# Decayed attention, a folded double product and routed experts on one core: the first combined product ahead of the last value products, and remainders on VectorE piece by piece

## The chip, the cores and the metric

The kernel runs on one core of a Trainium2 chip. The core has a matmul engine (TensorE, PE in the profile), three elementwise engines (VectorE, DVE; ScalarE, ACT; GpSimd, POOL) and SyncE (SP), whose queue issues the transfers that matter here. Each engine works through its own instructions in their order, and semaphores order the engines among each other. SBUF is the on-chip memory of 128 partitions, PSUM the banks that matmuls accumulate in. The metric is the device time of one launch in microseconds (us).

## What is computed

Attention over 4 batches of 8 heads, 576 tokens and 64 columns, with a decay from `f`; its output is the input x of a product of weights, and that the input of a layer with 8 experts. The reference, cut to what matters:

```python
cum = np.cumsum(np.log(np.clip(f, 0.0001, 1.0)), axis=-1)
scores = np.where(causal, -1e9, scale * q @ k.T + cum[:, None] - cum[None, :])
attn = np.exp(scores - scores.max(-1)); attn /= attn.sum(-1) + 1e-09
x = (attn @ v)                      # 2304 tokens x 512
a = x @ w1                          # w1, w2: 512 x 1024
b = x @ w2
h = a * b @ w3                      # 1024 x 1024
x = h @ w_out                       # 1024 x 512
# then: each token to the best of 8 experts, relu(x @ w1[e]) @ w2[e], scaled by its gates
```

## The kernel before

**Stages.** Attention works on 16 pairs of two heads (4 batches, 4 pairs each). A table, `START`, gives each step of a pair a due time in a period of 9.8, and steps of neighbouring pairs are written out in the order of those times; `AFTER` holds exceptions for the last pairs. Behind attention come the combined matrix C = w3 · w_out, the gated stage (a = x·w1, b = x·w2, their product, 8 column blocks f by 5 tiles of 512 tokens), the projection of that with C, the routing, and the experts.

**Products.** Every float32 matmul is done as three matmuls on rounded halves: hi·hi, hi·lo, lo·hi (lines 515 to 517, and 552 to 554 for the gated stage). C is 16 products (`hf`, j): two halves of its rows by 8 slices of the inner dimension, each of 12 matmuls of 128x512. The order is (0,0) to (0,3), (1,0) to (1,3), then (0,j), (1,j) for j = 4 to 7. At the end of each half its four PSUM banks (`wc`) are evicted, by ACT the `hi` (line 770) and by DVE the remainder (line 771). The first products of the gated stage are a00, b00, a01, b01 (tile 0, block f).

**Pieces.** The weights lie in DRAM as 64-bit words. `narrow` turns a piece of 128x512 into two halves of float32 in seven steps: 0 SP loads it (512 KB, line 449) into one of three buffers (tag `raw`); 1 ACT makes a scaled copy of the upper words (456); 2, 3, 4 DVE shifts and merges bits in place (458, 460, 462; 462 is the last to read the load buffer); 5 ACT rounds to `hi` (465); 6 POOL takes the remainder `lo` (467), or DVE where the argument `lows` says so. The pieces come in the order of the products: wo0, w00, wo1, ... (the first 12), then wo4, w04, w14, wo5, w05, w15, and so on to w17 (wo: slice j of w_out; w0j, w1j: of w3), then wa0, wb0, wa1, wb1, ... (blocks of w1 and w2). The tile that a piece has behind step 1 is called after it with a u: wo6u, w05u. Behind attention `convert` writes the steps of neighbouring pieces into the engines' queues, by a list of (step, how far ahead of the piece that is finished); `xsplit` does hi and remainder of the first tile of x (lines 572 and 573) between them.

**Ends of attention.** For a pair `pv` issues the value products (line 306), `add_blocks` adds probabilities on POOL (`ac`, line 297), `sums` brings their sums into the same PSUM tile (line 322), and `keep_sums` copies them out. At a batch's last pair `invert` loads the batch's sums (`z`, line 342), inverts them on DVE (344, 345) and stores them (`rz`, line 347).

Of the kernel before, what the change touches and what calls it, by code (L numbers as in the profile page):

```python
# [11 lines left out]
F32 = mybir.dt.float32  # L12
# [4 lines left out]
ALU = mybir.AluOpType  # L17
# [5 lines left out]
B, H, S, D = 4, 8, 576, 64  # L23
# [5 lines left out]
P = 128  # L29
# [9 lines left out]
AHEAD = 2  # L39

EARLY = 12
LOADS = 4

BLOCK = [(0, 192), (128, 832), (256, 1280), (384, 0), (512, 768)]
WIDTH = 1600
# [17 lines left out]

AFTER = {
    "K4_13": 4.4, "K4_14": 4.43, "K0_15": 15.6, "K0_16": 15.61, "K0_17": 15.62, "inputs": 11.36, "scores": 13.38,
    "K1_15": 18.5, "K1_16": 18.51, "K4_15": 18.52, "K0_18": 18.53, "K4_16": 18.54, "P0": 28.29, "P1": 28.3, "P2": 28.31,
    "P3": 28.32,
}

# [1 line left out]
def spread(nc, d, rz):  # L71

    for h in range(2):
        nc.sync.dma_start(out=d[64 * h:64 * h + 64], in_=rz[h:h + 1].broadcast_to([64, rz.shape[1]]))


def attention(nc, tc, ident, xT, rz, xs, wc, q, k, v, f):
# [6 lines left out]
    V, A, G, PE, SP = nc.vector, nc.scalar, nc.gpsimd, nc.tensor, nc.sync  # L84
    with (
# [70 lines left out]
        z = p1.tile([P, 512], BF16, name="warm")  # L156
# [16 lines left out]
        def tl(s, key, shape, dt=F32, bufs=2):  # L173
            if key in ("kh", "kl"):
                s[key] = KHs[key == "kl"][s["n"] % 2]
                return s[key][:, :S]
            if key not in s:
                pool = p2 if key in ("qr", "kr", "kh", "kl", "qh", "ql") else p3
                s[key] = pool.tile([P, *shape], dt, name=f"{key}_{s['n']}", tag=key, bufs=bufs)
            return s[key]  # L180
# [151 lines left out]
            b, pr = divmod(s["n"], NP)  # L332
            SP.dma_start(out=zd[pr, :, S * b:S * b + S].rearrange("h (i c) -> h i c", i=2), in_=s["zs"][0:P:32])

        def invert(s, step):

            if s["n"] % NP == NP - 1:
                b = s["n"] // NP
                z = tl(s, "z", (36,))
                view = lambda t: t.rearrange("x h n -> (x h) n")[:, S * b:S * b + S].rearrange("r (i c) -> r i c", c=36)  # L340
                if step == 0:
                    SP.dma_start(out=z, in_=view(zd))
                elif step == 1:
                    V.tensor_scalar(out=z, in0=z, scalar1=1e-9, scalar2=None, op0=ALU.add)
                    V.reciprocal(z, z)
                else:
                    SP.dma_start(out=view(rz), in_=z)
# [64 lines left out]
class Combined:  # L412


    def __init__(self, nc, tc, xpool, raw, wo, w3t):
        self.nc, self.tc, self.xpool, self.wo, self.w3t = nc, tc, xpool, wo, w3t
        self.pieces = [("o", 0), (0, 0), ("o", 1), (0, 1), ("o", 2), (0, 2), ("o", 3), (0, 3), (1, 0), (1, 1), (1, 2), (1, 3)]
        self.steps = [(hf, j) for hf in range(2) for j in range(4)]
        for j in range(4, 8):
            self.pieces += [("o", j), (0, j), (1, j)]  # L420
            self.steps += [(0, j), (1, j)]
        self.at = {x: i for i, x in enumerate(self.pieces)}
        self.queue = [self.narrow(f"w{x}{j}", wo[j] if x == "o" else w3t[x, j], self.slot(i)) for i, (x, j) in enumerate(self.pieces)]
        self.done, self.acc, self.spare = [0] * 7, {}, None
        self.raw = [raw.tile([P, 8, 512], F32, name=f"raw{i}", tag="u") for i in range(2)]
        self.units = [None] * 3
# [51 lines left out]
    def convert(self, n):  # L478

        for _ in range(n):  # L480
            x = self.done[6]
            for step, ahead in ((0, LOADS), (6, 1), (1, 4), (4, 2), (3, 3), (2, 4)):
                self.upto(step, x + ahead)

    def two(self, part):
# [34 lines left out]
def moe(nc, tc, ident, xT, rz, xs, xpool, raws, region, wc, w1, w2, gates, e1, e2, out):  # L520

    V, A, G, PE, SP = nc.vector, nc.scalar, nc.gpsimd, nc.tensor, nc.sync
    NCH = N // P
    with (
# [16 lines left out]
        def tmp(name):  # L541
            return st["work"].tile([P, 512], F32, name=name, tag="tmp", bufs=TMP if "moa" in st else 3)

        def split(src, hi, lo, lo_eng):
            G.tensor_scalar(out=hi, in0=src, scalar1=1.0, scalar2=1.0, op0=ALU.mult, op1=ALU.mult)  # L545
            lo_eng.tensor_tensor(out=lo, in0=src, in1=hi.bitcast(F32), op=ALU.subtract)  # L546
# [11 lines left out]
        def xparts(t):  # L558
            return [st["moa"].tile([P, 4, 512], F32R, name=f"{x}{t}", tag=x) for x in ("xh", "xl")]

        def xsplit(t, w, x, ks=range(4)):
            xh, xl = x
            for k in ks:
                xv = xT[:, k, 512 * t:512 * t + w]
                if t:
                    d = tmp(f"rz{t}{k}")[:, :w]
                    spread(nc, d, rz[k, :, 512 * t:512 * t + w])
                    G.tensor_tensor(out=xv, in0=xv, in1=d, op=ALU.mult)
                if t:
                    split(xv, xh[:, k, :w], xl[:, k, :w], V)  # L570
                else:
                    A.activation(out=xh[:, k, :w], in_=xv, func=ACTF.Copy)
                    G.tensor_tensor(out=xl[:, k, :w], in0=xv, in1=xh[:, k, :w].bitcast(F32), op=ALU.subtract)

        def gated(t, w, x, between):

# [170 lines left out]
        for f in range(8):  # L747
            for x, src, hi, lo in (("a", w1, w1h, w1l), ("b", w2, w2h, w2l)):
                spare = f % 2 if x == "b" and f > 1 else None
                wc.queue.append(wc.narrow(f"w{x}{f}", src[f], lambda hi=hi[:, f], lo=lo[:, f]: (hi, lo), spare, V if f else None))  # L750
        wc.banks(1, side="right")
        for hf, j in wc.steps:
            need = max(wc.at[hf, j], wc.at["o", j]) + 1
            wc.convert(max(0, need + AHEAD - wc.done[6]))
            if hf and j == 5:
                wc.first.close()
                st["moa"] = xpool.enter_context(tc.tile_pool(name="moa", bufs=1, side="right", reuse_waits="tile"))
                x = xparts(0)
            wc.product(hf, j)
            ks = XS.get((hf, j), ())  # L760
            if ks:
                xsplit(0, 512, x, ks)
            if 3 in ks:
                wc.spare = [xT[:, k:k + 2, 0:512] for k in (0, 2)]
            if j == 7:
                if hf == 0:
                    wch, wcl = (x.bitcast(F32R) for x in wc.raw)
                    st["unit"] += 2
                for f, ps in enumerate(wc.acc[hf]):
                    A.activation(out=wch[:, 4 * hf + f], in_=ps, func=ACTF.Copy)  # L770
                    V.tensor_tensor(out=wcl[:, 4 * hf + f], in0=ps, in1=wch[:, 4 * hf + f].bitcast(F32), op=ALU.subtract)  # L771
# [5 lines left out]
        gated(0, TT[0], x, iter(()))  # L777
        x = xparts(1)
        xsplit(1, TT[1], x)


# [31 lines left out]
        with tc.manual_schedule(engines={PE_E, POOL_E}):  # L813
            for t, w in list(enumerate(TT))[1:]:
# [3 lines left out]
                if t + 1 < len(TT):  # L818
                    x = xparts(t + 1)
# [290 lines left out]
        with tc.manual_schedule(engines={PE_E, DVE_E}):  # L1110
# [40 lines left out]
            x = next(fx)  # L1151
# [12 lines left out]
            for i in range(1, E):  # L1164
                nm, w = str(i), WIN[i]
# [17 lines left out]
                x = next(fx, None)  # L1183
# [9 lines left out]
                else:  # L1193
                    x = turned_piece("p", g2)
# [39 lines left out]
def program(shapes):  # L1234
    nc = bacc.Bacc("TRN2", target_bir_lowering=False, num_devices=1)
    a = {n: nc.dram_tensor(n, s, mybir.dt.from_np(t), kind="ExternalInput").ap() for n, (s, t) in shapes.items()}
    out = nc.dram_tensor("out", (N, DM), F32, kind="ExternalOutput").ap()
    with tile.TileContext(nc) as tc:
        with tc.tile_pool(name="keep", bufs=1) as keep, tc.tile_pool(name="raws", bufs=2, reuse_waits="tile") as raws, tc.tile_pool(name="div", bufs=1, space=DRAM) as div:
            rz = div.tile([NP, 2, N], F32, name="rz")  # L1240

            xs = div.tile([E * N, DM + 2], F32, name="xs")
            ident = keep.tile([P, P], F32, name="ident")
            keep.tile([P, 64], F32, name="shift")
            make_identity(nc, ident)
            xpool = ExitStack()
            xt = xpool.enter_context(tc.tile_pool(name="xt", bufs=1, side="right"))
            xT = xt.tile([P, NP, N], F32, name="xT")
            region = ExitStack()
            region.enter_context(tc.manual_schedule())  # L1250
            wc = Combined(nc, tc, xpool, raws, a["wo"], a["w3t"])
            attention(nc, tc, ident, xT, rz, xs, wc, a["q"], a["k"], a["v"], a["f"])
            moe(nc, tc, ident, xT, rz, xs, xpool, raws, region, wc, a["w1"], a["w2"], a["gates"], a["e1"], a["e2"], out)
            xpool.close()
    return nc
# [9 lines left out]
```

## Time and profile before

| what | value |
|---|---|
| median of 3 runs | 809.11 us (806.85 to 809.75) |
| the profiled execution | 808.69 us, of it the span 807.0 us |
| PE busy in the span | 778.8 us, 97% |
| DVE busy | 456.1 us, 57% |
| ACT, POOL busy | 280.0 us, 344.3 us |
| mean granted clock of PE | 0.997 of full speed |

The span runs from the profile's first instruction to its last; the execution's own time has what lies around it too. A row of a timeline gives start and duration, the engine, the line of the kernel, the operation, output and inputs, and in brackets how long the engine had been idle before it and what ended that.

### The profile page before, as it was taken

To read this page: it belongs to the slowest core of one execution; us is meant where nothing else is said; L and a number is where in the kernel's file an instruction comes from. 1 tells how busy PE (TensorE), PEld (TensorE's weight loads), DVE (VectorE), ACT (ScalarE), POOL (GpSimd) and SP (SyncE) were. 2 spreads that over 40 slices of the span, in tenths; PEclk is the share of its full clock that TensorE was granted. 3 is DMA by queue.
4 is the path that set the end of the run, shared out by engine and by line. 5 is a ranking of instruction groups with operands and counts; after the bars stand their busy time and mean duration, and the time that the engine had idled before them with its cause. 6 is when DMAs were issued, how large, how long until landed. Compare 5 with 4: busy or idle time off the path is not lost.

```text
span 807.0 us, 13835 instructions
## 1 busy us (share of the span) xinstructions
PE 778.8 (97%) x5171; PEld 644.0 (80%) x5173; DVE 456.1 (57%) x971; ACT 280.0 (35%) x536; POOL 344.3 (43%) x362
## 2 busy tenths in 40 slices
PE   8999999998999999999999999999899999999995
PEld 4666666676878887887888788898698999999983
DVE  7788888986899833340341322237367845446520
ACT  2566666553366412212222221223122222332221
POOL 6788888987460130230121011033445444443521
PEclk9999999999999999999999999999999999999998
DMA  3555767524545210110100010044676556456470
GB/s 108 164 161 182 229 213 242 155 61 144 171 170 185 78 41 14 53 39 1 53 16 17 21 40 0 2 132 144 205 230 212 173 194 198 166 189 222 143 264 29
DMA packets 40339, 102.12 MB, mean 127 GB/s; under 512 B 8610, under 2 KB 9314, under 8 KB 40016
## 3 DMA queue, kind: packets, MB, share of 16 engines
q1 hardware_dynamic: 37088, 91.46, 35.7%
q0 software_dynamic: 3184, 9.77, 3.2%
q8 instruction: 41, 0.67, 0.3%
q14 instruction: 26, 0.21, 0.1%
HBM read 84.47 MB, written 16.51 MB: 125 GB/s over the span
## 4 chain that ended last, share of the span: by engine, by line
PE 63%; DVE 14%; DMA 10%; issue 6%; POOL 4%; ACT 2%; SPq 0%; POOLq 0%; DVEq 0%; ACTq 0%
DVE junk L243 6%; PE b L552 4%; PE y L552 4%; PE y L554 4%; PE b L554 4%; PE a L552 4%; PE b L553 4%; PE y L553 4%; PE a L554 4%; PE a L553 4%; DMA out<-ot,id 3%; PE h L552 3%; PE h L554 3%; PE h L553 3%; POOL ac L297 2%
## 5 line engine op out<-in xcount | busy, mean ns | idle before, releaser
L582 DVE TENSOR_TENSOR ga<-b,ga 128x512 f32<-128x512 f32 (+1 forms) x40 | 25.4, 634 | 143.5 <-PE b L554 142.8
L711 POOL DMA_INDIRECT xs<-xr,pos x18 | 19.3, 1074 | 177.6 <-DVE pos L707 127.7
L243 DVE CUSTOM_DVE_ANT_0 junk<-x,tri 128x256 f32<-128x256 f32 (+3 forms) x128 | 62.6, 489 | 9.9 <-PE x L217 0.7
L552 PE MATMUL h<-gh,ah 128*128 128x320 f32 (+4 forms) x224 | 67.2, 300 | 0.0
L553 PE MATMUL h<-gl,ah 128*128 128x320 f32 (+4 forms) x224 | 66.9, 299 | 0.0
L554 PE MATMUL h<-gh,al 128*128 128x320 f32 (+4 forms) x224 | 66.9, 299 | 0.0
L552 PE MATMUL b<-xh,w2h 128*128 128x512 f32 (+1 forms) x160 | 60.1, 376 | 0.4 <-DVE raw L771 0.4
L552 PE MATMUL a<-xh,w1h 128*128 128x512 f32 (+1 forms) x160 | 59.8, 374 | 0.0
L554 PE MATMUL a<-xh,w1l 128*128 128x512 f32 (+1 forms) x160 | 59.1, 369 | 0.0
L554 PE MATMUL b<-xh,w2l 128*128 128x512 f32 (+1 forms) x160 | 59.0, 369 | 0.0
L553 PE MATMUL b<-xl,w2h 128*128 128x512 f32 (+1 forms) x160 | 58.9, 368 | 0.0
L553 PE MATMUL a<-xl,w1h 128*128 128x512 f32 (+1 forms) x160 | 58.8, 368 | 0.0
L285 POOL TENSOR_SCALAR_AFFINE_SELECT PT<-PT 128x256 f32<-128x256 f32 (+1 forms) x80 | 45.7, 586 | 28.7 <-ACT PT L279 26.5
L552 PE MATMUL y<-raw,gh 128*128 128x512 f32 x144 | 56.8, 395 | 0.0
L554 PE MATMUL y<-raw,gl 128*128 128x512 f32 x144 | 56.2, 390 | 0.0
L553 PE MATMUL y<-raw,gh 128*128 128x512 f32 x144 | 56.0, 389 | 0.0
L545 POOL TENSOR_SCALAR bh<-rb 128x1024 fp32r<-128x1024 f32 x28 | 35.7, 1277 | 47.4 <-DMA rb<-e 40.6
L584 ACT ACTIVATE gh<-ga 128x512 fp32r<-128x512 f32 (+1 forms) x40 | 23.6, 589 | 89.5 <-DVE ga L582 89.5
L991 DVE SCALAR_TENSOR_TENSOR hl<-h,hh 128x320 fp32r<-128x320 f32 (+4 forms) x56 | 25.5, 463 | 47.9 <-ACT hh L990 47.2
L306 PE MATMUL v<-PT,vr 128*64 128x448 f32 (+4 forms) x384 | 49.8, 396 | 1.1 <-ACT zs L329 1.1
L297 POOL TENSOR_TENSOR ac<-ac,PT 128x640 f32<-128x640 f32 (+1 forms) x32 | 45.6, 1424 | 1.6
L546 DVE TENSOR_TENSOR bl<-rb,bh 128x1024 fp32r<-128x1024 f32 x28 | 36.8, 1336 | 15.4 <-POOL bh L545 15.4
(611 smaller groups left out, 2165.8 us busy)
## 6 DMA issues: line engine op xcount, KB each, us to landing
ra<-e SPq DMA_DIRECT2D x28, 512.0 KB
rb<-e SPq DMA_DIRECT2D x28, 512.0 KB
w<-w3t SPq DMA_DIRECT2D x16, 512.0 KB
xs<-zero SPq DMA_DIRECT2D x8, 771.0 KB
vr<-v SPq DMA_DIRECT2D x16, 320.0 KB
kr<-k SPq DMA_DIRECT2D x16, 288.0 KB
qr<-q SPq DMA_DIRECT2D x16, 288.0 KB
wo<-wo SPq DMA_DIRECT2D x8, 512.0 KB
```

Source lines behind the costliest of these rows:

```text
L243: V.tensor_tensor_reduce(out=junk[:, :w], in0=s["x", i][:, 512 * h:512 * h + w] if i < 4 else s["x", i][:, 224:224 + S], in1=tri[:, 640 - ...
L285: G.affine_select(out=t, in_=t, pattern=[[0, 2], [1, w]], compare_op=ALU.is_ge, fill=0.0, base=0, channel_multiplier=-1,)
L297: G.tensor_tensor(out=acc[:, :, q0 - P:], in0=first if j == 1 else acc[:, :, q0 - P:], in1=src, op=ALU.add)
L306: PE.matmul(s["v"][HALF[h], 384 + q0:384 + q1], s["vr"][:, j, HALF[h]], place(s, j, h, q0, q1), start=(j == 0), stop=(j == 4 or q1 == P),)
L545: G.tensor_scalar(out=hi, in0=src, scalar1=1.0, scalar2=1.0, op0=ALU.mult, op1=ALU.mult)
L546: lo_eng.tensor_tensor(out=lo, in0=src, in1=hi.bitcast(F32), op=ALU.subtract)
L552: PE.matmul(ps, ah, bh, start=start and i == 0, stop=False)
L553: PE.matmul(ps, ah, bl, start=False, stop=False)
L554: PE.matmul(ps, al, bh, start=False, stop=stop and i == last)
L582: V.tensor_tensor(out=ga[:, :w], in0=pb[:, :w], in1=ga[:, :w], op=ALU.mult)
L584: A.activation(out=gh[:, f, :w], in_=ga[:, :w], func=ACTF.Copy)
L991: V.scalar_tensor_tensor(out=hl[:, f, :w], in0=ps[:, :w], scalar=0.0, in1=hh[:, f, :w].bitcast(F32), op0=ALU.max, op1=ALU.subtract)
```

## The change

Line numbers of the changed kernel are 3 to 5 higher: 458, 460, 462 become 461, 463, 465; 456 becomes 459; 465 and 467 become 468 and 470; 515 to 517 become 518 to 520; 770 and 771 become 775 and 776.

1. The first combined product (due time `P0`) is due at 22.9 and not at 28.29, just ahead of `p0` at 22.91, the first of the value products. It applies to the last pair alone.
2. The remainders of the pieces from wo4 on, of wa0 and wb0, and of x's first tile go to DVE; before, POOL took them.
3. `convert` has another list, and `LOADS` is 5: DVE's three steps and the remainder of a piece come one after another.
4. The last batch's sums are loaded into a tile that is kept, and DVE's inverse and the store of `rz` come at product (0,4).

```diff
-LOADS = 4
+LOADS = 5
...
-    "K1_15": 18.5, "K1_16": 18.51, "K4_15": 18.52, "K0_18": 18.53, "K4_16": 18.54, "P0": 28.29, "P1": 28.3, "P2": 28.31,
+    "K1_15": 18.5, "K1_16": 18.51, "K4_15": 18.52, "K0_18": 18.53, "K4_16": 18.54, "P0": 22.9, "P1": 28.3, "P2": 28.31,
...
-        def invert(s, step):
+        def invert(s, step, late=False):
...
-                z = tl(s, "z", (36,))
+                z = tl(s, "z", (36,)) if b < B - 1 else wc.last
...
+                elif b == B - 1 and not late:
+                    wc.late = lambda: (invert(s, 1, True), invert(s, 2, True))
...
-        self.queue = [self.narrow(f"w{x}{j}", wo[j] if x == "o" else w3t[x, j], self.slot(i)) for i, (x, j) in enumerate(self.pieces)]
+        self.queue = [self.narrow(f"w{x}{j}", wo[j] if x == "o" else w3t[x, j], self.slot(i), None, nc.vector if i >= 12 else None) for i, (x, j) in enumerate(self.pieces)]
...
-            for step, ahead in ((0, LOADS), (6, 1), (1, 4), (4, 2), (3, 3), (2, 4)):
+            for step, ahead in ((6, 1), (1, 4), (4, 2), (5, 2), (0, LOADS)):
...
-                    G.tensor_tensor(out=xl[:, k, :w], in0=xv, in1=xh[:, k, :w].bitcast(F32), op=ALU.subtract)
+                    V.tensor_tensor(out=xl[:, k, :w], in0=xv, in1=xh[:, k, :w].bitcast(F32), op=ALU.subtract)
...
-                wc.queue.append(wc.narrow(f"w{x}{f}", src[f], lambda hi=hi[:, f], lo=lo[:, f]: (hi, lo), spare, V if f else None))
+                wc.queue.append(wc.narrow(f"w{x}{f}", src[f], lambda hi=hi[:, f], lo=lo[:, f]: (hi, lo), spare, V))
...
+            if (hf, j) == (0, 4):
+                wc.late()
...
-            keep.tile([P, 64], F32, name="shift")
+            last = keep.tile([P, 64], F32, name="last")[:, :36]
```

The first place is PE's queue at the end of attention; `v` is the PSUM tile of a pair (2676 is pair 14's, 2739 or 2751 pair 15's), `cw` holds the first pieces. Before:

```order
L322 MATMUL v_2676<-PT_2543,ones 32x64 x2
L306 MATMUL v_2739<-PT_2659,vr_2695 64x128 x2
L306 MATMUL v_2739<-PT_2659,vr_2695 64x448 x4
L306 MATMUL v_2739<-PT_2659,vr_2695 64x320 x2
L306 MATMUL v_2739<-PT_2659,vr_2695 64x192 x2
L306 MATMUL v_2739<-PT_2659,vr_2695 64x64 x2
L322 MATMUL v_2739<-ac_2718,ones 32x288 x2
```

The twelve matmuls of product (0,0) stood behind the last of pair 15's sums. The same queue now:

```order
L322 MATMUL v_2676<-PT_2543,ones 32x64 x2
L518 MATMUL wc_2687<-cw 128x512
L519 MATMUL wc_2687<-cw 128x512
L520 MATMUL wc_2687<-cw 128x512
L518 MATMUL wc_2688<-cw 128x512
```

They stand between pair 14's sums and pair 15's value products.

The second place is DVE's queue in the middle of the conversion, around the pieces wo6 and w06. Before:

```order
L458 TENSOR_SCALAR wo6u<-wo6u 128x512
L462 SCALAR_TENSOR_TENSOR w15u<-w_2732,w15u 128x512
L460 SCALAR_TENSOR_TENSOR wo6u<-wo_2910,wo6u 128x512
L458 TENSOR_SCALAR w06u<-w06u 128x512
L462 SCALAR_TENSOR_TENSOR wo6u<-wo_2910,wo6u 128x512
L460 SCALAR_TENSOR_TENSOR w06u<-w_2931,w06u 128x512
L458 TENSOR_SCALAR w16u<-w16u 128x512
L462 SCALAR_TENSOR_TENSOR w06u<-w_2931,w06u 128x512
```

Now:

```order
L461 TENSOR_SCALAR wo6u<-wo6u 128x512
L463 SCALAR_TENSOR_TENSOR wo6u<-wo_2904,wo6u 128x512
L465 SCALAR_TENSOR_TENSOR wo6u<-wo_2904,wo6u 128x512
L470 TENSOR_TENSOR gl<-wo6u,gl 128x512
L461 TENSOR_SCALAR w06u<-w06u 128x512
L463 SCALAR_TENSOR_TENSOR w06u<-w_2913,w06u 128x512
L465 SCALAR_TENSOR_TENSOR w06u<-w_2913,w06u 128x512
L470 TENSOR_TENSOR gl<-w06u,gl 128x512
```

Three pieces were in work at a time; now a piece is done whole, its remainder among its steps.

The third place is DVE's queue from wb0 to the combined product's second eviction (`wc_2687` and the three behind it are the banks of the first half, `wc_2841` or `wc_2845` the first of the second; w2l is wb0's remainder). Before:

```order
L462 SCALAR_TENSOR_TENSOR wb0u<-wb_3043,wb0u 128x512
L460 SCALAR_TENSOR_TENSOR wa1u<-wa_3066,wa1u 128x512
L458 TENSOR_SCALAR wb1u<-wb1u 128x512
L771 TENSOR_TENSOR raw_78<-wc_2687,raw_77 128x512
L771 TENSOR_TENSOR raw_78<-wc_2688,raw_77 128x512
L771 TENSOR_TENSOR raw_78<-wc_2689,raw_77 128x512
L771 TENSOR_TENSOR raw_78<-wc_2690,raw_77 128x512
L462 SCALAR_TENSOR_TENSOR wa1u<-wa_3066,wa1u 128x512
L460 SCALAR_TENSOR_TENSOR wb1u<-wb_3075,wb1u 128x512
L458 TENSOR_SCALAR wa2u<-wa2u 128x512
L771 TENSOR_TENSOR raw_78<-wc_2845,raw_77 128x512
```

Now:

```order
L465 SCALAR_TENSOR_TENSOR wb0u<-wb_3024,wb0u 128x512
L576 TENSOR_TENSOR xl_2995<-xT,xh_2994 128x512
L776 TENSOR_TENSOR raw_78<-wc_2687,raw_77 128x512
L776 TENSOR_TENSOR raw_78<-wc_2688,raw_77 128x512
L776 TENSOR_TENSOR raw_78<-wc_2689,raw_77 128x512
L776 TENSOR_TENSOR raw_78<-wc_2690,raw_77 128x512
L470 TENSOR_TENSOR w2l<-wb0u,w2h 128x512
L461 TENSOR_SCALAR wa1u<-wa1u 128x512
L463 SCALAR_TENSOR_TENSOR wa1u<-wa_3049,wa1u 128x512
L465 SCALAR_TENSOR_TENSOR wa1u<-wa_3049,wa1u 128x512
L776 TENSOR_TENSOR raw_78<-wc_2841,raw_77 128x512
```

The last remainder of x is ahead of the evictions, and wb0's remainder with all of wa1's three steps between the two evictions. On ACT wb0's `hi` and the last `xh` stand ahead of the first eviction's ACT half, where wb0's `hi` stood behind all four.

## Rows read from the trace of the kernel before

**Rows 1.** The page: busy time of each engine, share of the span, instructions.

```profile
PE 778.8 (97%) x5171; PEld 644.0 (80%) x5173; DVE 456.1 (57%) x971; ACT 280.0 (35%) x536; POOL 344.3 (43%) x362
```

**Rows 2.** Busy time by stretch: length, engines, clock, DMA share, GB/s.

```profile
223.00:233.00 10.00, 10.00 (x46) 8.28 (x45) 10.00 (x7) 5.02 (x10) 9.46 (x7) 1.00 0.33 108
243.00:273.00 30.00, 30.00 (x133) 24.78 (x132) 30.00 (x56) 18.95 (x32) 0.06 (x1) 1.00 0.43 151
```

**Rows 3.** Timeline of PE: start, us, engine, line, operation, [idle before, releaser].

```profile
185.20 0.28 PE L322 MATMUL v<-PT,ones 128*32 128x64 f32 x4
186.58 2.92 PE L306 MATMUL v<-PT,vr 128*64 128x128 f32 x24 [1.10 <-ACT zs L329]
191.43 0.44 PE L322 MATMUL v<-ac,ones 128*32 128x288 f32 x2 [1.93 <-POOL ac L297]
192.15 0.50 PE L515 MATMUL wc<-cw 128*128 128x512 f32 x1
...
235.80 0.39 PE L552 MATMUL a<-xh,w1h 128*128 128x512 f32 x1
...
239.13 0.50 PE L552 MATMUL b<-xh,w2h 128*128 128x512 f32 x1 [0.45 <-DVE raw L771]
...
242.46 0.50 PE L554 MATMUL a<-xh,w1l 128*128 128x512 f32 x1
```

**Rows 4.** Timeline of POOL.

```profile
190.05 1.32 POOL L297 TENSOR_TENSOR ac<-ac,PT 128x384 f32<-128x384 f32 x1
...
209.92 1.61 POOL L467 TENSOR_TENSOR gl<-wo6u,gl 128x512 fp32r<-128x512 f32 x1 [1.87 <-ACT gl L465]
```

**Rows 5.** Timeline of SP's queue.

```profile
194.91 0.64 SPq L342 DMA_DIRECT2D z<-zd  x1
...
198.82 0.46 SPq L449 DMA_DIRECT2D wo<-wo  x1
...
208.67 0.33 SPq L449 DMA_DIRECT2D wo<-wo  x1
```

**Rows 6.** Timeline of DVE.

```profile
197.19 0.55 DVE L344 TENSOR_SCALAR z<-z 128x36 f32<-128x36 f32 x1 [4.07 <-DMA z<-zd]
...
199.27 0.69 DVE L460 SCALAR_TENSOR_TENSOR w05u<-w,w05u 128x512 int32<-128x512 int32 x1
...
206.83 1.77 DVE L462 SCALAR_TENSOR_TENSOR wo6u<-wo,wo6u 128x512 int32<-128x512 int32 x1
...
209.36 0.43 DVE L458 TENSOR_SCALAR w16u<-w16u 128x512 int32<-128x512 int32 x1 [0.15 <-ACT w16u L456]
209.70 0.69 DVE L462 SCALAR_TENSOR_TENSOR w06u<-w,w06u 128x512 int32<-128x512 int32 x1
...
225.89 1.78 DVE L462 SCALAR_TENSOR_TENSOR wa0u<-wa,wa0u 128x512 int32<-128x512 int32 x1
...
238.40 2.47 DVE L771 TENSOR_TENSOR raw<-wc,raw 128x512 fp32r<-128x512 f32 x4
...
241.73 0.68 DVE L467 TENSOR_TENSOR w1l<-wa1u,w1h 128x512 fp32r<-128x512 f32 x1
```

**Rows 7.** Timeline of ACT.

```profile
203.15 0.66 ACT L456 ACTIVATE wo6u<-wo 128x512 f32<-128x512 f32 x1 [5.57 <-DMA wo<-wo]
...
212.10 0.66 ACT L456 ACTIVATE wo7u<-wo 128x512 f32<-128x512 f32 x1 [2.26 <-DMA wo<-wo]
212.67 0.62 ACT L465 ACTIVATE gl<-w06u 128x512 fp32r<-128x512 f32 x1
...
232.33 2.02 ACT L770 ACTIVATE raw<-wc 128x512 fp32r<-128x512 f32 x4
```

**Rows 8.** Busy time by stretch, as in rows 2, behind PE's last work.

```profile
798.00:799.00 1.00, 0.43 (x4) 0.00 (x0) 0.00 (x0) 0.39 (x1) 0.00 (x0) 1.00 0.00 0
802.00:803.00 1.00, 0.00 (x0) 0.00 (x0) 0.00 (x0) 0.00 (x0) 0.00 (x0) 0.50 0.00 0
```

More of the change, by code (lines that the diff above doesn't have):

```diff
@@ L412, with __init__ @@
 class Combined:
-    def __init__(self, nc, tc, xpool, raw, wo, w3t):
+    def __init__(self, nc, tc, xpool, raw, wo, w3t, last):
+        self.last = last
         self.nc, self.tc, self.xpool, self.wo, self.w3t = nc, tc, xpool, wo, w3t
@@ L1250, in program @@
             region.enter_context(tc.manual_schedule())
-            wc = Combined(nc, tc, xpool, raws, a["wo"], a["w3t"])
+            wc = Combined(nc, tc, xpool, raws, a["wo"], a["w3t"], last)
             attention(nc, tc, ident, xT, rz, xs, wc, a["q"], a["k"], a["v"], a["f"])
```

## Prediction

> **What bounds the kernel now.** First the page's line of engine totals: TensorE (PE) is busy for 97% of the span, VectorE (DVE) for 57% [rows 1]. Such a share hides stages, so next come slices around the change. In the slice at the end of the conversion and in the one inside the gated stage PE and DVE are both full, the second for 30 us together [rows 2]. The reader should see two things: PE sets the time here, and DVE has no spare time before 273 us to catch up if it falls behind.
>
> PE's rows show where PE is not full. It waits 1.10 us before pair 15's value products and 1.93 us before its sums, starts the combined product at 192.15 and has no wait until the gated stage begins at 235.80; there it waits 0.45 us at b00 [rows 3]. The 16 products are 192 matmuls in 235.80 − 192.15 = 43.65 us, 0.2273 us each, so one product is 2.73 us.
>
> **The change, part by part.**
>
> Product (0,0) ahead of the value products. It is 2.73 us of work with operands long in SBUF. PE comes free at 185.48, behind pair 14's last sums [rows 3]; the product runs to 188.2, over the wait of 1.10. The value products take 2.92 us, to 191.1. The sums need POOL's last `ac`, which ends at 190.05 + 1.32 = 191.37 as before [rows 4], so they still start at 191.43, and the next product at 192.15. Only 15 are left there: PE would be ready for a00 at 235.80 − 2.73 = 233.08. The gain is 2.73 us, and the small waits at the start of the gated stage could go too.
>
> The last inverse in the kept tile. Before, SP issued the load of z at 194.91, DVE waited 4.07 us for it, and only behind the store of rz did wo6's load go out, at 198.82 [rows 5, 6]. Now two loads stand ahead of that store, and wo6's goes at 194.91 + 0.64 = 195.55: 3.3 us sooner. Behind the store on SP is w16's load, which has to wait for its buffer longer than that; I price the store at nothing.
>
> Remainders on DVE. Eighteen subtractions move: twelve pieces of wo and w3, wa0, wb0 and four pieces of x. One takes POOL 1.61 us and DVE 0.68 us [rows 4, 6], some 0.6 when it follows without a gap: 18 × 0.6 = 10.8 us more for DVE. Against it stand DVE's long rows: beside POOL a step with two inputs took 1.77 and 1.78 us, otherwise 0.69 [rows 6]. With POOL silent these should go, 1.1 us each. In busy time the exchange is about even; the answer lies in the order.
>
> DVE's order. Before, three pieces stood interleaved on DVE, and the remainder, which must wait for ACT's `hi`, was on POOL with nothing urgent behind it. Now DVE runs one piece whole, L461, L463, L465 and the remainder L470, and the next piece's steps stand behind that. L470 waits for `hi` (L468) on ACT. On ACT the scaled copy (L459) of the piece two further on is ahead of that `hi`. That copy waits for its load, and with three load buffers this load is issued when L465 of the piece before has ended. This is a ring over two pieces. From rows: issue 0.05 (an estimate, small beside the rest); landing to the start of the copy 212.10 − 208.67 = 3.43, taken as 3.5 [rows 5, 7]; copy 0.57, from its start to that of the `hi` behind it, and `hi` 0.62 [rows 7]; remainder 0.6; the three steps 0.43 + 0.69 + 0.69 = 1.81, and 0.04 between them [rows 6]. Sum 7.2 us for two pieces, 3.6 for one, of which DVE works 2.45. Before, wo6u ended at 206.83 + 1.77 = 208.60 and wa0u, six pieces on, at 225.89 + 1.78 = 227.67 [rows 6]: 3.2 for one.
>
> Follow the end of L465. wo6's load goes at 195.55 and lands at 199.05; copy, `hi` and remainder of w05 and w15's three steps bring w15 to 202.8. By the ring w06 ends at 210.0, wo7 at 217.2, w17 at 224.4; two remainders of x (1.2) and an `xh` (0.5) stand between, so 226.1. wa0 is bound by ACT and DVE themselves: `hi`, `xh`, a remainder of x, w17's remainder and three steps, 0.62 + 0.6 + 0.6 + 0.6 + 1.85: 230.4 (before 227.67). Product (1,7) needs w17's remainder, at about 228.5, and is due at 230.35: the 15 products hide the ring, with 1.9 us of cover left.
>
> What is late next. wa0's end frees the buffer for wb1's load: issued 230.4, its copy on ACT starts at 233.95. On ACT, behind it, stand wb0's `hi`, the last `xh` and the evictions of the combined product (2.02 us for four [rows 7]); on DVE the last remainder of x and the evictions' other half (2.47 for four, 0.62 each [rows 6]). The first eviction ends at 233.95 + 0.6 + 0.65 + 0.55 + 0.6 + 0.62 = 237.0. a00 writes the PSUM bank that it frees, so PE waits from 233.08: 3.9 us, where it had no wait. Then DVE: three evictions 1.85, wb0's remainder 0.6, wa1's three steps 1.85, and across wa1's `hi` and the next eviction's first half on ACT (0.55 + 0.5) that eviction's second half 0.7: 242.5 to 243.05, of which I take the later, since each step here follows another engine's. b00 needs that bank, with PE ready at 237.0 + 2.73 = 239.7: 3.3 us. Then three evictions 1.85, wb1's three steps 1.85, two shifts 0.7, wa1's remainder 0.45: 247.9. a01's third matmul reads it, with PE ready at 243.05 + 14 × 0.2273 = 246.2: 1.7 us. It starts at 247.9, against 242.46 before [rows 3]: all behind it is 5.4 us later. From there the steps stand in the order of before and DVE is full [rows 2], so nothing comes back, and later stages shift as a whole.
>
> By terms: −2.73 (product) − 0.7 (the 0.45 at b00 and small steps of before) + 3.9 + 3.3 + 1.7 = +5.4, rounded. The profiled execution took 808.69 us, so 814.1; the runs' median, 809.11, is 0.42 above it, so 814.5.
>
> Bounds. Below: loads soon enough for the first eviction to be through by 233.08, and DVE's order alone counts. From there b00 comes 6.05 us later (243.05 − 237.0), a01's third matmul another 4.85, at 243.98: +1.5. Above: landings as with two loads in flight, 203.15 − 198.82 = 4.33 [rows 5, 7], five on the chain (wo6, w16, w07, wa0, wb1), 0.9 each: +4.5 more. I take 3.5, since in the ring one load is mostly alone.
>
> [...]
>
> **The rivals.**
>
> The other side: the plan works. DVE is rid of the 1.78 us steps, loads start 3.3 us sooner, PE finds everything ready: −2.73 − 0.7, 805.3, with the 0.42 805.7. For it: DVE works 2.45 us per piece in the ring and waits for the rest, so a shorter ring would show at once. Against it: the first eviction would have to end near 229.4, right behind its product's last matmul, 7.6 us sooner than I find; over five landings that is 1.5 each, and it decides below a landing of 2.0 us, where the shortest of the loads read here took 3.43. Chance 0.08. [...]
>
> Order alone costs: the lower bound, 808.69 + 1.5 + 0.42 = 810.6. It wants 3.9 us off the chain, 0.8 per landing or as much elsewhere on it, such as steps that overlap where I set them end to end. Chance 0.15.
>
> Loads land late or the clock falls: 814.5 + 4.5 = 819, half of it with half of the loads. For it: 4.33 was seen. Chance 0.12.
>
> **How the numbers follow.** My forecast has 0.65, by itself 812.5 to 816.5. A measurement of this kernel can tell about 0.5%, 4.05 us, from no change: below 805.06 or above 813.16. Faster: half of the first rival, 0.04. Same: its other half, the second rival (0.15) and a fifth of the forecast (0.13), 0.32. Slower: the rest of the forecast, 0.52, and the late loads, 0.12, together 0.64. The range of 810.0 to 819.0 takes in the second rival and the late loads and leaves out the first and the fringes.
>
> **What would show it.** Right: the first product at about 185.5 and PE's wait of 1.10 gone; L461 to L465 at 0.4 to 0.7 us throughout; wo6's load issued near 195.6; L465 of pieces two apart ending 7.2 us apart, with gaps on DVE between L465 and L470 of one piece; wb1's load near 230.4; PE waiting 3.9 and 3.3 us at a00 and b00 for evictions (L776) and 1.7 in a01 for L470. Wrong: pieces that end under 2.7 us apart, a00 near 233, or PE waiting inside the products already, which would mean a chain longer than mine.

## The result, and the profile after

The changed kernel took 815.60 us in the median of four runs (814.58 to 819.13), the kernel before 808.14 us beside it: a ratio of 1.0092, 95% interval 1.0072 to 1.0111. It is 7.5 us slower; the forecast was 5.4 against the profiled execution, 814.5 in all, and the range 810.0 to 819.0. The profiled execution of the changed kernel took 815.23 us, 6.54 more than that of before.

The page of the changed kernel, span and engine totals, answers to [rows 1]:

```profile
span 813.6 us, 13836 instructions
...
PE 781.6 (96%) x5171; PEld 645.7 (79%) x5173; DVE 453.1 (56%) x989; ACT 279.6 (34%) x536; POOL 321.5 (40%) x344
```

DVE has 18 instructions more and is busy 3.0 us less. The long rows beside POOL are gone, as the plan of the change would have it; and yet the span is 6.6 us longer. The total does not show why. PE's timeline around the change does, for the places of [rows 3]:

```profile
185.20 0.50 PE L518 MATMUL wc<-cw 128*128 128x512 f32 x1
...
191.29 0.44 PE L322 MATMUL v<-ac,ones 128*32 128x288 f32 x2 [0.20 <-POOL ac L297]
192.01 0.50 PE L518 MATMUL wc<-cw 128*128 128x512 f32 x1
...
237.32 0.79 PE L555 MATMUL a<-xh,w1h 128*128 128x512 f32 x1 [4.22 <-DVE raw L776]
...
243.37 0.50 PE L555 MATMUL b<-xh,w2h 128*128 128x512 f32 x1 [1.55 <-DVE raw L776]
...
248.22 0.50 PE L557 MATMUL a<-xh,w1l 128*128 128x512 f32 x1 [1.38 <-DVE w1l L470]
```

Product (0,0) starts at 185.20; the wait of 1.10 is gone, that of 1.93 is down to 0.20, and the next product starts at 192.01 where it was at 192.15. So 2.73 us were gained, as said. Then PE stands for 4.22 us at a00, 1.55 at b00 and 1.38 in a01, each time for DVE. The third matmul of a01 is at 248.22, 5.76 us later than in [rows 3].

The steps that PE waits for are found by following DVE's queue back. DVE's timeline, the L465 of three pieces, each with the remainder that follows it:

```profile
202.09 0.69 DVE L465 SCALAR_TENSOR_TENSOR w15u<-w,w15u 128x512 int32<-128x512 int32 x1
203.94 0.69 DVE L470 TENSOR_TENSOR gl<-w15u,gl 128x512 fp32r<-128x512 f32 x1 [1.16 <-ACT gl L468]
...
205.73 0.69 DVE L465 SCALAR_TENSOR_TENSOR wo6u<-wo,wo6u 128x512 int32<-128x512 int32 x1
207.73 0.69 DVE L470 TENSOR_TENSOR gl<-wo6u,gl 128x512 fp32r<-128x512 f32 x1 [1.31 <-ACT gl L468]
...
209.52 0.69 DVE L465 SCALAR_TENSOR_TENSOR w06u<-w,w06u 128x512 int32<-128x512 int32 x1
```

In front of both remainders DVE stands idle for more than a microsecond, for ACT's `hi`; from w15 to wo7 this wait is 0.95 to 1.31 us. ACT's timeline tells what ACT was doing:

```profile
206.50 0.67 ACT L459 ACTIVATE w16u<-w 128x512 f32<-128x512 f32 x1 [2.60 <-DMA w<-w3t]
207.08 0.62 ACT L468 ACTIVATE gl<-wo6u 128x512 fp32r<-128x512 f32 x1
```

Nothing: it waited 2.60 us for the load of w16, whose copy stands ahead of wo6's `hi`. And SP's timeline, when that load was issued (the rows are the loads of wo6, w06, w16 and wb1):

```profile
195.54 0.38 SPq L452 DMA_DIRECT2D wo<-wo  x1
...
199.21 0.33 SPq L452 DMA_DIRECT2D w<-w3t  x1
...
202.84 0.33 SPq L452 DMA_DIRECT2D w<-w3t  x1
...
230.77 0.33 SPq L452 DMA_DIRECT2D wb<-w  x1
```

At 202.84, when w15's L465 had ended (202.09 + 0.69 = 202.78) and so freed a buffer. That is the whole ring: L465 of one piece (w15), the load into the buffer that it frees (w16), that load's copy, the `hi` behind the copy (wo6), its remainder on DVE, the next piece's three steps, and so the L465 of the piece two further on (w06). From w15's end to w06's (210.21) it took 7.43 us, from w06's to wo7's 7.17.

### The profile page after: what moved, and what is told of

The parts are those of the page before. It is cut to its first block, busy times and chain, and to the rows that moved or that the text cites. A ratio compares the mean times of both kernels' runs of the same rounds, so it can differ in the third digit from the quotient of the medians.

```text
span 813.6 us, 13836 instructions
## 1 busy us (share of the span) xinstructions
PE 781.6 (96%) x5171; PEld 645.7 (79%) x5173; DVE 453.1 (56%) x989; ACT 279.6 (34%) x536; POOL 321.5 (40%) x344
## 4 chain that ended last, share of the span: by engine, by line
PE 66%; DVE 15%; DMA 8%; issue 7%; ACT 2%; SPq 1%; POOL 0%; DVEq 0%; POOLq 0%; ACTq 0%
DVE junk L243 7%; PE y L557 4%; PE y L555 4%; PE y L556 4%; PE b L555 4%; PE a L555 4%; PE a L557 4%; PE b L557 4%; PE b L556 4%; PE a L556 4%; DMA out<-ot,id 3%; PE h L555 3%; PE h L557 3%; PE h L556 3%; PE q L555 2%
## 5 line engine op out<-in xcount | busy, mean ns | idle before, releaser
L571 POOL TENSOR_TENSOR xT<-xT,rz 128x512 f32<-128x512 f32 (+1 forms) x16 | 21.5, 1345 | 87.8 <-ACT w2h L468 87.8
L548 POOL TENSOR_SCALAR bh<-rb 128x1024 fp32r<-128x1024 f32 x28 | 37.6, 1342 | 45.3 <-DMA rb<-e 39.5
```

## Experiments

All are told by the ratio to the kernel before, run beside them, and by three places in PE's timeline. The execution of attention varies by some 3 us (pair 15's sums start at 191.25 in e2 and at 194.40 in e8), so the table counts from the start of pair 15's sums (191.43 in before, 191.29 in the changed kernel).

| kernel | ratio to before (95%) | a00 | b00 | a01, third matmul |
|---|---|---|---|---|
| before | 1 | 44.37 | 47.70 | 51.03 |
| changed | 1.0092 (1.0072 to 1.0111) | 46.03 | 52.08 | 56.93 |
| e1 product's move alone | 0.9984 (0.9966 to 1.0003) | 41.84 | 45.77 | 49.10 |
| e11 the same, more rounds | 0.9991 (0.9975 to 1.0007) | 41.93 | 45.86 | 49.19 |
| e2 changed without the product's move | 1.0100 (1.0059 to 1.0142) | 47.25 | 53.31 | 58.16 |
| e3 changed, hi ahead of the copy | 1.0056 (1.0039 to 1.0073) | 43.05 | 49.66 | 54.56 |
| e4 changed, old order of steps | 0.9992 (0.9978 to 1.0007) | 42.30 | 46.83 | 50.16 |
| e5 changed, inverse as before | 1.0141 (1.0120 to 1.0162) | 49.77 | 55.82 | 60.68 |
| e6 changed, remainders on POOL | 1.0009 (0.9991 to 1.0026) | 41.65 | 45.53 | 50.38 |
| e7 changed, remainder a piece later | 0.9996 (0.9979 to 1.0014) | 41.65 | 44.72 | 49.57 |
| e8 old order, store and remainder moved | 0.9969 (0.9957 to 0.9982) | 41.65 | 44.55 | 47.86 |
| e9 e8 without the product's move | 0.9997 (0.9982 to 1.0012) | 44.42 | 47.14 | 50.31 |
| e10 e7, wa1's remainder sooner | 0.9983 (0.9969 to 0.9997) | 41.66 | 44.73 | 48.03 |
| e12 remainders on DVE alone | 0.9996 (0.9982 to 1.0011) | 44.39 | 47.11 | 50.40 |

**The ring.** e3 takes the landing out of it and leaves all else:

```diff
-            for step, ahead in ((6, 1), (1, 4), (4, 2), (5, 2), (0, LOADS)):
+            for step, ahead in ((6, 1), (4, 2), (5, 2), (1, 4), (0, LOADS)):
```

> The changed kernel with one edit in the order of steps: a piece's hi stands on ACT ahead of the scaled copy of the piece two further on, so that it no longer stands behind that copy's load. Loads, remainders on DVE and DVE's order stay. Theory (the ring goes through the landing): the ring is cut, a piece takes hi 0.6, remainder 0.6 and three steps 1.85 in a row, 3.1 us in place of 3.6; a00 near 234, b00 near 240.4, a01's third near 245.2, 3 us faster than the changed kernel. Rival (DVE simply has too much work with the remainders): no difference, a01's third at 248.

DVE's timeline of e3, the L465 of three pieces in a row and a remainder:

```profile
201.70 0.69 DVE L465 SCALAR_TENSOR_TENSOR w15u<-w,w15u 128x512 int32<-128x512 int32 x1
203.09 0.69 DVE L470 TENSOR_TENSOR gl<-w15u,gl 128x512 fp32r<-128x512 f32 x1 [0.70 <-ACT gl L468]
...
204.88 0.69 DVE L465 SCALAR_TENSOR_TENSOR wo6u<-wo,wo6u 128x512 int32<-128x512 int32 x1
...
208.06 0.69 DVE L465 SCALAR_TENSOR_TENSOR w06u<-w,w06u 128x512 int32<-128x512 int32 x1
```

A piece takes 3.18 us where it took 3.6, and the wait ahead of a remainder is 0.70, ACT's `hi` alone. The rival, that DVE has too much work, falls: no work was taken from it. The gain is 2.4 us at a01 (54.56 against 56.93) where 3 were expected, and 0.0036 or 2.9 us by the ratios. Behind a wait of 3.58 us at b00 the clock fell to 0.50, and b00 took 4.44 us to a01's start, where e8's took 2.86.

e7 takes the remainder's wait away altogether, by putting the next piece's steps ahead of it:

```diff
-            for step, ahead in ((6, 1), (1, 4), (4, 2), (5, 2), (0, LOADS)):
+            for step, ahead in ((4, 2), (6, 1), (5, 2), (1, 4), (0, LOADS)):
```

> The changed kernel with another list of steps: DVE's three steps of the next piece stand ahead of the remainder of this one, and hi ahead of the copy two pieces on. Theory (a remainder that need not wait costs DVE its 0.6 us alone): a piece every 2.5 us, DVE without gaps, a00 near 233 without a wait, b00 near 236.2 after half a us, a01's third near 241.1 after 1.7 us: 1.4 us faster than before, 7 faster than the changed kernel. Rival (DVE cannot take the remainders): a01's third later than 242.5.

DVE's timeline of e7:

```profile
203.33 0.69 DVE L465 SCALAR_TENSOR_TENSOR wo6u<-wo,wo6u 128x512 int32<-128x512 int32 x1
203.94 0.68 DVE L470 TENSOR_TENSOR gl<-w15u,gl 128x512 fp32r<-128x512 f32 x1
204.54 0.42 DVE L461 TENSOR_SCALAR w06u<-w06u 128x512 int32<-128x512 int32 x1
204.99 0.69 DVE L463 SCALAR_TENSOR_TENSOR w06u<-w,w06u 128x512 int32<-128x512 int32 x1
205.72 0.69 DVE L465 SCALAR_TENSOR_TENSOR w06u<-w,w06u 128x512 int32<-128x512 int32 x1
206.33 0.69 DVE L470 TENSOR_TENSOR gl<-wo6u,gl 128x512 fp32r<-128x512 f32 x1
```

No bracket is left: in these rows DVE never waits, and a piece takes 2.39 us. With the same instructions on the same engines as the changed kernel, a01 is 7.4 us sooner (49.57 against 56.93). By the ratios, 0.9996 against 1.0092, it is about 7.8 us, and the kernel is level with before. The 1.4 us that it was to be faster than before are there in the rows (a01 49.57 against 51.03) and not in the ratio; its trace has a fall of the clock in the experts (0.58 from 570 to 574), of which the part on the size tells.

e4 sets the old list of steps, and loads four ahead, into the changed kernel.

```diff
-LOADS = 5
+LOADS = 4
...
-            for step, ahead in ((6, 1), (1, 4), (4, 2), (5, 2), (0, LOADS)):
+            for step, ahead in ((0, LOADS), (6, 1), (1, 4), (4, 2), (3, 3), (2, 4)):
```

> The changed kernel with the order of steps and the look-ahead of loads of the kernel before (three pieces interleaved on DVE); the product's move, the remainders on DVE and the late inverse stay. Theory (the order is what costs): hi stands ahead of the copies on ACT, and on DVE two other steps stand between a piece's last merge and its remainder, so neither waits; a piece takes DVE's own 2.45 us, a00 at 233 without a wait, b00 near 236.8, a01's third near 240.1: 2.3 us faster than before, 8 faster than the changed kernel. Rival (remainders on DVE are the cost, in whatever order): slower than before, a01's third near 248.

It lost the 7 us too: 0.9992. But the 2.3 us against before did not come; a01 is 0.87 sooner than in before. SP's timeline of e4 shows a load that goes out late:

```profile
195.98 0.38 SPq L452 DMA_DIRECT2D wo<-wo  x1
201.26 0.60 SPq L349 DMA_DIRECT2D rz<-last  x1
201.97 0.87 SPq L452 DMA_DIRECT2D w<-w3t  x2
```

In this order the store of `rz`, which waits for DVE's inverse, stands ahead of w06's load, and the two loads behind it go out together at 201.97, 10.2 us after the sums, where the changed kernel had w06's out after 7.9 (199.21). Whether this is what the 2.3 us were lost to is not shown by e4 alone; e8, below, bears on it.

**Does a late load go through to the end?** e5 gives the changed kernel the inverse of before.

```diff
-                elif b == B - 1 and not late:
+                elif False:
...
-            if (hf, j) == (0, 4):
-                wc.late()
```

> The changed kernel with the last inverse as it was: DVE inverts the sums where they are loaded, and rz's store stands ahead of wo6's load. Theory (the ring carries a delay of one load to its end, piece by piece): wo6's load 3.3 us later, every piece from w15 on 3.3 later, PE waits already in the last products, a01's third matmul 3 to 3.7 us later than in the changed kernel. Rival (a late load is caught up again within the fifteen products): the time of the changed kernel.

DVE waits for z again ahead of w05 (4.01 us): w05's merge ends 11.73 us after the sums, 3.87 later than in the changed kernel (7.86). w15 is 3.54 later, wa0 3.71, a01's third matmul 3.75 (60.68 against 56.93). The ring carried the delay nearly one to one from w05 to wa0, over nine pieces. PE's timeline of e5:

```profile
229.18 0.50 PE L520 MATMUL wc<-raw,raw 128*128 128x512 f32 x1 [0.19 <-DVE raw L470]
...
233.54 0.50 PE L520 MATMUL wc<-raw,raw 128*128 128x512 f32 x1 [1.11 <-DVE raw L470]
...
241.93 0.80 PE L555 MATMUL a<-xh,w1h 128*128 128x512 f32 x1 [5.83 <-DVE raw L774]
```

PE waits inside the products now: the cover of 1.9 us over product (1,7) was used up. So the late inverse, by itself, is worth some 3.7 us in the changed kernel; by the ratios, 1.0141 against 1.0092, it is 4.0.

**The remainders.** e6 puts them back on POOL in the changed kernel; e12 makes the opposite of the same three edits in the kernel before.

```diff
-... self.slot(i), None, nc.vector if i >= 12 else None) for i, (x, j) in enumerate(self.pieces)]
+... self.slot(i), None, None) for i, (x, j) in enumerate(self.pieces)]
...
-                    V.tensor_tensor(out=xl[:, k, :w], in0=xv, ...
+                    G.tensor_tensor(out=xl[:, k, :w], in0=xv, ...
...
-... (hi, lo), spare, V))
+... (hi, lo), spare, V if f else None))
```

> The changed kernel with the remainders back on POOL; order, look-ahead, late inverse and the product's move stay. Theory (the ring closes only because the remainder, which waits for hi, stands on DVE's queue): pieces follow each other at what loads and DVE allow, 2 to 3 us, although DVE's steps beside POOL take 1.78 us again; no wait at a00, a01's third matmul at 240.5 to 242.5, 0 to 2 us faster than before and 6 to 8 faster than the changed kernel. Rival (the order of the loads or of the copies costs, wherever the remainder runs): a01's third near 246 to 248.

> The kernel before with one edit: the eighteen remainders on DVE; order of steps, look-ahead, inverse and product as before. Theory (the place of the remainder costs nothing where it need not wait; the 10.8 us more work are paid by steps that no longer take 1.78 us beside POOL): b00 within 1 us of before, no change in time beyond 1 us. Rival (more work on a full DVE): some us slower, up to the changed kernel's 7.

Neither can be told from before: 1.0009 and 0.9996. In e6 the list of the changed kernel no longer makes the ring, since no DVE step waits for `hi`; the 0 to 2 us that e6 was to be faster than before show as 0.65 us at a01 and not in the ratio. PE has no wait at a00, and DVE's steps beside POOL are long again, 1.80 us against 0.69; DVE's timeline of e6:

```profile
207.42 0.69 DVE L465 SCALAR_TENSOR_TENSOR w06u<-w,w06u 128x512 int32<-128x512 int32 x1
208.03 0.42 DVE L461 TENSOR_SCALAR w16u<-w16u 128x512 int32<-128x512 int32 x1
208.49 1.80 DVE L463 SCALAR_TENSOR_TENSOR w16u<-w,w16u 128x512 int32<-128x512 int32 x1
```

In e12 the remainders on DVE cost nothing that the ratio tells in the old order. So neither the list nor the place of the remainders makes the ring alone; the two together do. That the list costs nothing else is not shown: e6 has the product's move and the late inverse beside it, and its a01 is still 2.5 us behind that of e8.

**What the product's move is worth.** e1 and e11 make it alone in the kernel before; e2 undoes it in the changed kernel, e9 in e8.

```diff
-    ... "P0": 28.29, "P1": 28.3, "P2": 28.31,
+    ... "P0": 22.9, "P1": 28.3, "P2": 28.31,
```

> The changed kernel with product (0,0) back behind the value products. Theory (the conversion on DVE and ACT ends last, PE waits for it): a00 at 237.3 as in the changed kernel, after a wait of about 1.5 in place of 4.2; b00 at 243.4, a01's third at 248.2; the time of the changed kernel within 1 us. If the clock stays at 1.00 behind the shorter wait, b00's wait grows to about 3.3 and the end stays. Rival (the product's 2.73 us are gained in the changed kernel too): a00 near 240 and 2.7 us slower than the changed kernel.

> The kernel before with one edit: product (0,0) due at 22.9, ahead of the last pair's value products; remainders, order and inverse as before. Theory (behind attention DVE's order, not PE, sets when the gated stage may start): the product fills PE's wait of 1.10 us and the 15 others end near 233.1, but b00 still waits for the eviction that DVE ends at 239.1, so a00 may start early while b00 stays at 239.1 and a01's third matmul at 242.5: 0 us, within 0.5 us of before. Rival (the product's move is worth its own length): b00 near 236.4 and 2.7 us faster than before.

> The kernel of e1 once more, in more rounds, since its interval there held 0 and reached to 2.7 us faster. Theory: b00 waits for DVE's eviction, 0 to 1 us faster than before. Rival: 2.7 us faster.

> The kernel of e8 with product (0,0) back behind the value products. Theory (the product's move is worth its 2.73 us only where the conversion no longer ends last): PE has no wait at a00 and b00, the start of the gated stage follows PE, b00 at 47.2 us behind pair 15's sums where e8 had it at 44.5: 2 to 2.7 us slower than e8, 0 to 0.7 faster than before. Rival (the product's place is worth nothing there either): as e8, 2.5 faster than before.

In the changed kernel the ratios show no worth: 1.0100 against 1.0092. But e2's interval reaches to 1.0142 and so holds the rival too, which would be 1.0126; the rows decide. SP's, ACT's and PE's timelines of e2:

```profile
195.49 0.38 SPq L452 DMA_DIRECT2D wo<-wo  x1
...
200.09 0.66 ACT L459 ACTIVATE wo6u<-wo 128x512 f32<-128x512 f32 x1 [3.50 <-DMA wo<-wo]
...
238.50 0.50 PE L555 MATMUL a<-xh,w1h 128*128 128x512 f32 x1 [2.73 <-DVE raw L776]
```

PE still waits for DVE at a00, 2.73 us where it was 4.22, so PE was not last. a00 is 1.22 us later after the sums than in the changed kernel, and 1.06 of that is one landing: 4.60 us for wo6 where the changed kernel had 3.54. A single late load went through to the end here as well.

Alone (e1, e11) it brought 0.9984 and 0.9991, intervals that hold 1; the 2.7 us of the rival would be 0.9967, outside the second. PE is at a00 2.5 us sooner, and waits 0.92 and 0.90 us at b00 for DVE's eviction. Both traces have the clock's fall in the experts (0.65 from 574 to 578 in e1, 0.64 from 570 to 574 in e11), so a part of what a01 gained may be lost again there. My own expectation is not met in full: b00 was to stay, and is 1.8 to 1.9 us sooner after the sums in both traces. In those DVE ended the merge of w17 at 29.45 and 29.55 after the sums, in before at 31.39, with the same order; where POOL's remainders met DVE's steps was different. Whether the earlier product brings that about, or the one trace of before was a late one, stays open.

e8 is the version in which the product counts. It sets the old list with loads five ahead, moves the store of `rz` and takes wa1's remainder ahead of wb1's steps:

```diff
-            for step, ahead in ((6, 1), (1, 4), (4, 2), (5, 2), (0, LOADS)):
+            for step, ahead in ((0, LOADS), (6, 1), (1, 4), (4, 2), (3, 3), (2, 4)):
...
-            if (hf, j) == (0, 4):
+            if (hf, j) == (0, 6):
                 wc.late()
...
+        wc.upto(6, 27)
         wc.upto(4, 28)
```

> The changed kernel with the old order of steps, as in e4, and three more edits: loads five ahead, the late inverse at product (0,6) in place of (0,4), so that its store does not hold a load on SP (in e4 w06's load stood behind it until 201.97), and wa1's remainder ahead of wb1's steps. Theory (in e4 the load behind the store cost the rest): w06's load issued near 199 to 200, no wait at a00 and b00 or under 1 us, a01's third near 239.7 to 241: 1 to 2.7 us faster than before. Rival (what is lost in e4 lies with DVE): as e4, under 1 us faster than before.

w06's load goes out 7.2 us after the sums. The kernel is faster than both: 806.28 us in the median, 0.9969 of before (0.9957 to 0.9982), some 2.5 us. PE's timeline of e8, from the sums of pair 15, has no bracket at a00 or b00:

```profile
194.40 0.44 PE L322 MATMUL v<-ac,ones 128*32 128x288 f32 x2
...
236.05 0.39 PE L555 MATMUL a<-xh,w1h 128*128 128x512 f32 x1
...
238.95 0.50 PE L555 MATMUL b<-xh,w2h 128*128 128x512 f32 x1
```

a00 is at 41.65 after the sums, where PE is ready. Against e4, e8 has three edits at once (loads five ahead, the store, wa1's remainder), and no run parts them. Without the product's move (e9) the same kernel has a00 at 44.42, again without a wait; PE's timeline of e9:

```profile
191.31 0.44 PE L322 MATMUL v<-ac,ones 128*32 128x288 f32 x2 [1.92 <-POOL ac L297]
...
235.73 0.39 PE L555 MATMUL a<-xh,w1h 128*128 128x512 f32 x1
```

It is back at 0.9997: 2.77 us by the rows, 0.0028 or 2.3 us by the ratios. That is the product's 2.73 us, paid out where DVE and ACT are done before PE.

> The kernel of e7 with wa1's remainder ahead of wb1's steps. Theory (in e7 that order alone kept the last wait of 1.4 us, and DVE is full behind it, so that part of the wait comes back a block later): no wait in a01, up to 1.2 us in a02; 0 to 0.8 us faster than e7, 1 to 2.5 faster than before. Rival (DVE full: the whole wait moves): as e7.

e10 (`wc.upto(6, 27)` added to e7) has no wait in a01, and 0.94 us at the same matmul of a02, as said; its a01 is 1.54 us sooner than e7's. Its ratio, 0.9983, lies 0.0013 or 1.1 us below e7's, where 0 to 0.8 was expected; the two intervals overlap, so the times do not tell e10 from e7.

## Why the prediction was right, step by step

The product. Said: 2.73 us gained, a00 ready at 233.08. It ended its products at about 233.1; PE's wait of 4.22 ahead of 237.32 counts back to 233.10.

The ring. Said: 7.2 us for two pieces. Measured between the ends of L465 of pieces two apart: w05 to wo6 7.27, w15 to w06 7.43, wo6 to w16 7.22, w06 to wo7 7.17, w16 to w07 7.19. w15, w06, wo7, w17 and wa0 were to end at 202.8, 210.0, 217.2, 226.1 and 230.4; they ended at 202.78, 210.21, 217.38, 226.33 and 230.69. wb1's load was to go at 230.4 and went at 230.77.

The three waits. Said 3.9, 3.3 and 1.7; measured 4.22, 1.55 and 1.38. The first and the last are the chain's, 0.3 us off. The second is smaller because a00 itself took longer: the clock fell. The changed kernel's busy time by stretch, with columns as in [rows 2]:

```profile
236.00:237.00 1.00, 0.00 (x0) 0.00 (x0) 1.00 (x2) 1.00 (x3) 0.00 (x0) 1.00 1.02 416
...
238.00:239.00 1.00, 1.00 (x4) 0.81 (x3) 1.00 (x3) 0.46 (x1) 0.00 (x0) 0.50 0.22 82
239.00:240.00 1.00, 1.00 (x3) 0.76 (x3) 0.99 (x3) 0.00 (x0) 0.00 (x0) 0.50 0.00 0
...
241.00:242.00 1.00, 0.82 (x4) 0.34 (x2) 0.44 (x1) 0.52 (x1) 0.00 (x0) 1.00 0.00 0
```

The eighth column is the granted clock. It is 1.00 in the slice in which PE still stands, 0.50 while a00 runs, and 1.00 again at 241. a00's twelve matmuls take 4.5 us, 237.32 to 243.37 − 1.55 = 241.82, where e8 has 2.9 from a00 to b00. With e8's 2.9 the wait at b00 would have been about 3.2 (an estimate: 243.37 − 237.32 − 2.9), where 3.3 was said; b00 has to wait for its bank anyway, so its wait shrinks and nothing is lost. Neither the sum of the prediction nor that of its rival with late loads or a falling clock (814.5 + 4.5) has a term for the clock; here the fall to 0.50 took some 1.6 us (4.5 − 2.9) from b00's wait.

The size. Said +5.4 on the profiled execution, measured +6.54: 5.76 at a01, and some 0.8 that came later. These 0.8 are in no term of the sum. They come with a second fall of the clock, in the experts, in the changed kernel's busy time by stretch:

```profile
579.00:580.00 1.00, 1.00 (x4) 0.81 (x3) 0.00 (x0) 0.55 (x1) 0.64 (x1) 0.50 0.77 213
```

PE's timeline there, the changed kernel's two rows and then the same two of before:

```profile
575.94 0.50 PE L555 MATMUL oA<-bhm,hhA 128*128 128x512 f32 x1 [1.25 <-POOL bhm L548]
...
585.30 0.39 PE L557 MATMUL oA<-bhm,hlA 128*128 128x512 f32 x1
```

```profile
570.37 0.50 PE L552 MATMUL oA<-bhm,hhA 128*128 128x512 f32 x1 [1.39 <-POOL bhm L545]
...
578.11 0.39 PE L554 MATMUL oA<-bhm,hlA 128*128 128x512 f32 x1
```

The changed kernel is 5.57 us behind ahead of the fall and 7.19 behind it; 0.6 of these 1.6 us come back right after (586.68 against 580.10), where PE in before waits 0.84 us for a load. In the trace of before the clock stays at 1.00 there. That the change brings this fall about is not shown: of the fourteen traces of this study four have a fall between 570 and 582 (the changed kernel, e1, e7 and e11), and e2 and e5, with waits at the changed kernel's three places, and e3, at two of them, have none. The mean clock of all four executions of the changed kernel is 0.992 or 0.993, as in the traced one, so the others may have a second fall as well; why it comes stays open. The rest, from 6.54 to the 7.5 of the medians, is that the execution of before that was profiled lies 0.55 above its median and that of after 0.37 below its own.

The rivals. That the plan works on the changed kernel's own order (805.7) had its condition put rightly: the ring would have had to be shorter. Put in another order the same plan does work (e8 and e10, 0.9969 and 0.9983; e7 is level), and one remainder is shorter on DVE, 0.69 us against POOL's 1.61 [rows 4], but that decides nothing here: moved alone (e12), the remainders changed the time by 0.9996, no change that can be told. The statement that in busy time the exchange is about even holds: 456.1 us before, 453.1 after. The bound by DVE's order alone (810.6) would have wanted shorter landings, and the landings were as taken: 202.84 to 206.50 and 195.54 to 199.08 give 3.66 and 3.54, where 3.5 was taken; the issue, an estimate of 0.05, was 202.84 − 202.78 = 0.06. A late landing is the 4.60 of e2, of one load.

Where the expected gain went: 2.73 us were gained in the products and none of it reached the gated stage, because DVE and ACT, not PE, were last there (e2, and e8 against e9); and the new order put a load's landing into DVE's queue once for every two pieces.

## What to carry to other kernels

Before a step that waits for another engine is moved onto a busy in-order queue, follow what that wait stands behind on the other engine; here it was a copy that waited for a load that waited for a buffer that the busy queue frees, and the loop's length times the number of pieces, from rows alone, gave each piece's end to 0.3 us. Such a ring can be cut by order alone, with the same instructions on the same engines: let the step wait behind one more piece's work (e7, a01 7.4 us sooner), or put its producer ahead of whatever waits for a load (e3, 2.4 us). And a gain in an engine's own work is paid out where that engine is last: here PE's 2.73 us showed as 0.9969 against 0.9997 where PE was last (e8, e9), and not, 1.0092 against 1.0100, where DVE and ACT were (the changed kernel, e2). Look at who ends the wait at the next stage's first instruction before counting it.

## What the runs showed of the hardware that was not expected

At the kernel's end the clock fell to 0.50 while PE stood idle [rows 8]. It also fell behind waits of 2.73, 1.22 and 0.81 us, and there PE was already at work again. In e2 PE stood for 2.73 us ahead of a00 at 238.50; busy time by stretch of e2:

```profile
238.00:239.00 1.00, 0.50 (x2) 0.46 (x3) 1.00 (x3) 1.00 (x4) 0.00 (x0) 1.00 1.03 399
239.00:240.00 1.00, 1.00 (x4) 0.75 (x4) 1.00 (x3) 0.64 (x2) 0.00 (x0) 0.52 0.44 170
```

In e8's trace it fell in attention, behind a wait of 1.22 us for a load, which ended at 128.84:

```profile
128.00:129.00 1.00, 0.16 (x2) 0.16 (x4) 0.94 (x5) 0.37 (x1) 0.00 (x0) 1.00 1.04 396
129.00:130.00 1.00, 1.00 (x12) 1.00 (x14) 0.99 (x3) 0.78 (x2) 0.00 (x0) 0.56 1.13 343
```

That execution's attention ended 3.0 us later than before's, and it was the longest of e8's ten (809.11; the others 804.91 to 808.57). e1's trace has the same fall (0.91 from 128 to 130, 0.50 from 130 to 132) behind a wait of 0.81 us at that place, and attention 2.9 us late; in before this wait is 0.44, and the clock stays at 1.00. The length of the last wait does not decide by itself: in e4, waits of 0.47 and 1.52 us at a00 and b00 brought no fall (1.00 from 238 to 239, and 0.998 in the mean of the execution), and in the experts before has 1.39 and 0.76 us without a fall, where the changed kernel has 1.25 and 0.76 with one.

A part of the spread of this kernel's times goes with the granted clock. Of the 35 executions of before that were run beside e9 to e12, the 17 with a mean clock of 0.997 or more took 807.6 to 808.9 us, and the 14 with 0.995 or less 809.1 to 812.1. How much of that difference is the clock itself, and how much the waits ahead of the falls, no run parts.
